# RMSNorm over 16,384 rows of 640 on one core: other tile sizes and row layout, scaling in place, a different share of squares, halved last stores

## The chip, the cores and the metric

One core of a Trainium2 chip runs the whole kernel. The metric is device time in microseconds of one execution, given as the median of several runs. The kernel before: 115.51 us, the median of 4 runs (115.45 to 115.58).

## What is computed

Every row of `x` (512 x 32 rows of 640 bf16 numbers) is divided by its root mean square and multiplied by a vector `g` of 640.

```python
B, S, D = 512, 32, 640
def reference(x, g):
    rms = jnp.sqrt((x * x).mean(axis=-1, keepdims=True) + 1e-6)
    return x / rms * g
```

`x` is 20.97 MB and the output as much; `g` is small.

## The kernel before

The 16,384 rows are cut into 16 tiles of 1,024 rows: 128 partitions with R = 8 rows each. A tile is one contiguous block of memory, 1.31 MB, of which a partition holds 10,240 contiguous bytes (lines 34 to 40). One Python loop over the tiles (line 62) is unrolled; a scheduler orders each engine's instructions at build time, mostly by program order, and puts in the semaphore waits. Each engine then works through its own list in that order. The work of one tile:

- SP issues the load of the tile into `x_sb` (line 66); the pool has 5 buffers, so the load of tile t+5 waits until tile t has been read for the last time.
- ACT (ScalarE) squares `kt` of the 8 rows, one instruction a row, which also sums the row into a column of `ms_a` in PSUM (line 73), and takes the root of these sums (line 80). `kt` follows the pattern 7, 7, 6, 7, 7, 7, 6, 7, which makes 108 rows of 128 per partition.
- DVE (VectorE) does the remaining `8 - kt` rows with a custom multiply-and-sum into `ms_d` (line 91), 20 in all; ACT takes their root as well (line 101).
- DVE takes the reciprocal of the 8 roots (line 108), multiplies the tile by `g` in two instructions of 4 rows into `xg` (line 113), and scales each row by its own reciprocal into `o_sb`, 8 instructions (line 122). `xg` has 2 buffers, `o_sb` has 3.
- POOL (GpSimd) issues the store of the tile, one DMA of 1.31 MB (line 130).

Before the loop ACT issues the load of `g`, broadcast to all partitions (line 52), and DVE writes the constant `eps_sb` (line 55).

All 16 DMA engines serve both the load queue of SP and the store queue of POOL.

Of the kernel before, what the change touches and what calls it, by code (L numbers as in the profile page):

```python
# [2 lines left out]

# [4 lines left out]


@with_exitstack  # L10
def kernel(
    ctx: ExitStack,
    tc: tile.TileContext,
    x: bass.AP,
    g: bass.AP,
    out: bass.AP,
):
    nc = tc.nc
    P = nc.NUM_PARTITIONS
    fp32 = mybir.dt.float32  # L20
    bf16 = mybir.dt.bfloat16
    Square = mybir.ActivationFunctionType.Square
    Sqrt = mybir.ActivationFunctionType.Sqrt
    mult = mybir.AluOpType.mult
    add = mybir.AluOpType.add

    xf = x.flatten_outer_dims()
    of = out.flatten_outer_dims()
    N, D = xf.shape
    assert N % P == 0  # L30
    rows_per_part = N // P
    eps = 1e-6

    R = 8
    while rows_per_part % R != 0:
        R -= 1
    T = rows_per_part // R

    xv = xf.rearrange("(t p r) d -> t p r d", p=P, r=R)
    ov = of.rearrange("(t p r) d -> t p r d", p=P, r=R)  # L40

    consts = ctx.enter_context(tc.tile_pool(name="consts", bufs=1))
    xpool = ctx.enter_context(tc.tile_pool(name="xpool", bufs=5))
    xgpool = ctx.enter_context(tc.tile_pool(name="xgpool", bufs=2))
    opool = ctx.enter_context(tc.tile_pool(name="opool", bufs=3))
    junkp = ctx.enter_context(tc.tile_pool(name="junk", bufs=2))
    psum_j = ctx.enter_context(tc.tile_pool(name="psum_j", bufs=2, space=bass.MemoryType.PSUM))
    psum_s = ctx.enter_context(tc.tile_pool(name="psum_s", bufs=2, space=bass.MemoryType.PSUM))
    statp = ctx.enter_context(tc.tile_pool(name="stats", bufs=3))

    g_sb = consts.tile([P, D], g.dtype, name="g_sb")
    nc.scalar.dma_start(out=g_sb[:], in_=g.partition_broadcast(P))

    eps_sb = consts.tile([P, 1], fp32, name="eps_sb")
    nc.vector.memset(eps_sb[:], eps)  # L55

    inv_sqrt_d = 1.0 / math.sqrt(D)
    inv_d = 1.0 / D

    kt_pattern = [7, 7, 6, 7, 7, 7, 6, 7]  # L60

    for t in range(T):
        kt = min(R, kt_pattern[t % len(kt_pattern)])
        nd = R - kt
        x_sb = xpool.tile([P, R, D], bf16, name="x_sb")
        nc.sync.dma_start(out=x_sb[:], in_=xv[t])

        rstd = statp.tile([P, R], fp32, name="rstd")
        if kt > 0:
            ms_a = psum_s.tile([P, R], fp32, name="ms_a")  # L70
            for r in range(kt):
                pj = psum_j.tile([P, D], fp32, name="pj")
                nc.scalar.activation(  # L73
                    out=pj[:],
                    in_=x_sb[:, r, :],
                    func=Square,
                    scale=inv_sqrt_d,
                    accum_out=ms_a[:, r : r + 1],
                )
            nc.scalar.activation(  # L80
                out=rstd[:, :kt],
                in_=ms_a[:, :kt],
                func=Sqrt,
                bias=eps_sb[:],
                scale=1.0,
            )
        if nd > 0:
            ms_d = statp.tile([P, R], fp32, name="ms_d")
            for r in range(kt, R):
                junk = junkp.tile([P, D], bf16, name="junk_dve")  # L90
                nc.vector.tensor_tensor_reduce(  # L91
                    out=junk[:],
                    in0=x_sb[:, r, :],
                    in1=x_sb[:, r, :],
                    scale=inv_d,
                    scalar=0.0,
                    op0=mult,
                    op1=add,
                    accum_out=ms_d[:, r : r + 1],
                )  # L100
            nc.scalar.activation(  # L101
                out=rstd[:, kt:R],
                in_=ms_d[:, kt:R],
                func=Sqrt,
                bias=eps_sb[:],
                scale=1.0,
            )
        nc.vector.reciprocal(out=rstd[:], in_=rstd[:])  # L108

        xg = xgpool.tile([P, R, D], bf16, name="xg")  # L110
        H = R // 2
        for h in range(2):
            nc.vector.tensor_tensor(  # L113
                out=xg[:, h * H : (h + 1) * H, :],
                in0=x_sb[:, h * H : (h + 1) * H, :],
                in1=g_sb[:, None, :].to_broadcast([P, H, D]),
                op=mult,
            )

        o_sb = opool.tile([P, R, D], bf16, name="o_sb")  # L120
        for r in range(R):
            nc.vector.tensor_scalar(  # L122
                out=o_sb[:, r, :],
                in0=xg[:, r, :],
                scalar1=rstd[:, r : r + 1],
                scalar2=None,
                op0=mult,
            )

        nc.gpsimd.dma_start(out=ov[t], in_=o_sb[:])  # L130


# [1 line left out]
_INS = ['x', 'g']  # L134
_OUTS = [((512, 32, 640), 'bfloat16')]


# [23 lines left out]
```

## Time and profile before

| | |
|---|---|
| median of 4 runs | 115.51 us (115.45 to 115.58) |
| the profiled execution's own time | 115.45 us |
| its span, first to last instruction | 113.7 us |
| DVE busy | 99.1 us, 217 instructions |
| ACT busy | 88.2 us, 250 instructions |
| POOL busy | 8.8 us, 20 instructions |
| moved by DMA | 42.14 MB |

All rows of the profile are from one execution, and their times count from the first instruction; 1.75 us of the execution's own time lie outside that span. A row of a timeline begins with its start and its duration in us, then engine, line, operation, output and input with their shapes, and a count where rows of one kind were merged; in brackets stands the idle time of the engine before it and what ended that. A row of a group has, behind the bar, the busy time in us and the mean duration of one in ns. A row of the waits says which engine waited for what: total us, times, and the longest where it is given. In the rows of 40 slices each digit is the busy share of one slice in tenths. PSUM and SBUF are the two on-chip memories; an engine name with a q behind it is that engine's queue.

### The profile page before, as it was taken

What the parts mean: (1) busy time and instruction counts of PE and PEld (TensorE: products, weight loads), DVE (VectorE), ACT (ScalarE), POOL (GpSimd) and SP (SyncE); (2) the same over time, 40 slices, a digit from 0 to 9 for tenths busy, and PEclk for the clock granted to TensorE, in tenths of its full rate; (3) what the DMA queues carried; (4) which work ended last, traced back from release to release, by engine and by line L of the source; (5) the groups of instructions that cost most, each with busy time, mean ns of one, the idle gap of its engine ahead of it and who ended that gap; (6) DMA issues with size and microseconds to landing.
All of it is one profiled execution on the core that took longest, in us unless ns stands there. A gap on an engine that the chain in (4) does not pass through costs nothing.

```text
span 113.7 us, 584 instructions
## 1 busy us (share of the span) xinstructions
DVE 99.1 (87%) x217; ACT 88.2 (78%) x250; POOL 8.8 (8%) x20
## 2 busy tenths in 40 slices
DVE  0019999999999999999999999999999999999700
ACT  4019999999999998989899999998989898710000
POOL 0000001101010101011010100101010101010100
DMA  4899999999999999999999999999999973809182
GB/s 66 313 352 440 414 443 422 436 422 428 404 418 435 425 436 422 432 429 418 436 425 436 429 429 429 424 429 407 425 425 436 414 335 126 346 0 404 58 346 115
DMA packets 4756, 42.14 MB, mean 371 GB/s; under 512 B 528, under 2 KB 656, under 8 KB 656
## 3 DMA queue, kind: packets, MB, share of 16 engines
q1 hardware_dynamic: 2304, 20.97, 44.8%
q0 software_dynamic: 2304, 20.97, 43.9%
q10 hardware_dynamic: 144, 0.16, 0.6%
q14 instruction: 4, 0.03, 0.1%
HBM read 21.14 MB, written 20.97 MB: 370 GB/s over the span
## 4 chain that ended last, share of the span: by engine, by line
issue 45%; DVE 26%; ACT 12%; DMA 6%; POOL 4%; POOLq 1%
DVE o_sb L122 13%; DVE xg L113 11%; ACT pj L73 10%; DMA x_sb<-in_x_dram 6%; POOL out_dram L130 4%; DVE junk_dve L91 2%; ACT L101 1%; DVE rstd L108 1%; POOLq L156 0%; ACT rstd L101 0%; ACT rstd L80 0%; DVE ms_d L91 0%; POOLq L130 0%
## 5 line engine op out<-in xcount | busy, mean ns | idle before, releaser
L73 ACT ACTIVATE pj<-x_sb 128x640 f32<-128x640 bf16 x108 | 76.1, 707 | 7.5 <-DMA x_sb<-in_x_dram 5.5
L113 DVE TENSOR_TENSOR xg<-x_sb,g_sb 128x2560 bf16<-128x2560 bf16 x32 | 46.7, 1472 | 0.0
L122 DVE TENSOR_SCALAR o_sb<-xg,rstd 128x640 bf16<-128x640 bf16 x128 | 39.3, 382 | 0.0
L91 DVE CUSTOM_DVE_ANT_0 junk_dve<-x_sb 128x640 bf16<-128x640 bf16 x20 | 16.1, 809 | 7.1 <-DMA x_sb<-in_x_dram 7.1
L130 POOL DMA_DIRECT2D out_dram<-o_sb x16 | 8.6, 540 | 98.9 <-DVE o_sb L122 98.9
L73 ACT ACTIVATION_READ_ACCUMULATOR pj<-x_sb 128x1 f32 x108 | 14.4, 133 | 0.0
L101 ACT ACTIVATE rstd<-ms_d,eps_sb 128x1 f32<-128x1 f32 (+1 forms) x16 | 4.8, 300 | 5.3 <-DVE ms_d L91 5.3
L80 ACT ACTIVATE rstd<-ms_a,eps_sb 128x7 f32<-128x7 f32 (+1 forms) x16 | 4.3, 267 | 0.0
L108 DVE RECIPROCAL rstd<-rstd 128x8 f32<-128x8 f32 x16 | 3.2, 198 | 0.2 <-ACT rstd L80 0.2
L73 ACT ACT_TABLE_LOAD x1 | 1.3, 1283 | 1.2 <-PEq L145 1.2
L91 DVE DVE_READ_ACCUMULATOR2_ANT ms_d<- 128x1 f32 x20 | 1.7, 84 | 0.0
L101 ACT ACT_TABLE_LOAD x1 | 1.3, 1283 | 0.0
L55 DVE MEMSET eps_sb<- 128x1 f32 x1 | 0.1, 59 | 0.8 <-PEq L145 0.8
L145 POOL MEMSET const-float32-0.0<- 128x1 f32 x1 | 0.1, 98 | 0.2 <-issue 0.2
L145 POOL MEMSET const-bfloat16-1.0<- 128x1 bf16 x1 | 0.1, 101 | 0.0
L145 POOL MEMSET const-float32-1.0<- 128x1 f32 x1 | 0.1, 98 | 0.0
L145 POOL MEMSET const-uint8-127<- 128x1 uint8 x1 | 0.1, 98 | 0.0
## 6 DMA issues: line engine op xcount, KB each, us to landing
x_sb<-in_x_dram SPq DMA_DIRECT2D x16, 1280.0 KB, 10.6
out_dram<-o_sb POOLq DMA_DIRECT2D x16, 1280.0 KB, 11.4
g_sb<-in_g_dram ACTq DMA_DIRECT2D x1, 160.0 KB, 7.4
```

What stands on the lines that cost most here:

```text
L55: nc.vector.memset(eps_sb[:], eps)
L73: nc.scalar.activation(out=pj[:], in_=x_sb[:, r, :], func=Square, scale=inv_sqrt_d, accum_out=ms_a[:, r : r + 1],)
L80: nc.scalar.activation(out=rstd[:, :kt], in_=ms_a[:, :kt], func=Sqrt, bias=eps_sb[:], scale=1.0,)
L91: nc.vector.tensor_tensor_reduce(out=junk[:], in0=x_sb[:, r, :], in1=x_sb[:, r, :], scale=inv_d, scalar=0.0, op0=mult, op1=add, accum_out= ...
L101: nc.scalar.activation(out=rstd[:, kt:R], in_=ms_d[:, kt:R], func=Sqrt, bias=eps_sb[:], scale=1.0,)
L108: nc.vector.reciprocal(out=rstd[:], in_=rstd[:])
L113: nc.vector.tensor_tensor(out=xg[:, h * H : (h + 1) * H, :], in0=x_sb[:, h * H : (h + 1) * H, :], in1=g_sb[:, None, :].to_broadcast([P, H, ...
L122: nc.vector.tensor_scalar(out=o_sb[:, r, :], in0=xg[:, r, :], scalar1=rstd[:, r : r + 1], scalar2=None, op0=mult,)
L130: nc.gpsimd.dma_start(out=ov[t], in_=o_sb[:])
L145: nc = _bacc.Bacc("TRN2", target_bir_lowering=False, num_devices=1)
```

## The change

- The rows are laid out otherwise: each partition now holds 128 consecutive rows of `x`, and a tile is a stretch of these. So a tile in memory is 128 pieces of 10,240 bytes, 163,840 bytes apart, for loads and stores alike.
- There are 17 tiles: 4 rows, 15 times 8, and 4 rows per partition.
- The pool of `x_sb` has 8 buffers instead of 5, that of `o_sb` 6 instead of 3; `xg` goes.
- A root of a single column is taken on ACT ahead of the loop.
- The rows that ACT squares follow a running share of 112/128, rounded: 4, then 6 and 8 in turn, and 4 for the last tile. Tiles in which ACT has all rows have no second root.
- The multiplication by `g` is one instruction per tile, into `o_sb`; the scaling reads and writes `o_sb` in place.
- The stores of the last three tiles are two DMAs each, of half the rows.

```diff
-    R = 8
-    while rows_per_part % R != 0:
-        R -= 1
-    T = rows_per_part // R
-
-    xv = xf.rearrange("(t p r) d -> t p r d", p=P, r=R)
-    ov = of.rearrange("(t p r) d -> t p r d", p=P, r=R)
+    xv = xf.rearrange("(p r) d -> p r d", p=P)
+    ov = of.rearrange("(p r) d -> p r d", p=P)
...
+        sizes = [4] + [8] * 15 + [4]
...
-    xpool = ctx.enter_context(tc.tile_pool(name="xpool", bufs=5))
-    xgpool = ctx.enter_context(tc.tile_pool(name="xgpool", bufs=2))
-    opool = ctx.enter_context(tc.tile_pool(name="opool", bufs=3))
+    xpool = ctx.enter_context(tc.tile_pool(name="xpool", bufs=8))
+    opool = ctx.enter_context(tc.tile_pool(name="opool", bufs=6))
...
+    warm = consts.tile([P, 1], fp32, name="warm")
+    nc.scalar.activation(out=warm[:], in_=eps_sb[:], func=Sqrt)
...
-    kt_pattern = [7, 7, 6, 7, 7, 7, 6, 7]
+    act_frac = 112.0 / 128.0
+    kt_list = []
+    acc = 0.0
+    done = 0
+    for s in sizes:
+        acc += s * act_frac
+        kt = int(round(acc)) - done
+        kt = max(0, min(s, kt))
+        kt_list.append(kt)
+        done += kt
...
-        x_sb = xpool.tile([P, R, D], bf16, name="x_sb")
-        nc.sync.dma_start(out=x_sb[:], in_=xv[t])
+        x_sb = xpool.tile([P, RMAX, D], bf16, name="x_sb")
...
+            nc.sync.dma_start(out=x_sb[:, :Rt, :], in_=xv[:, r0 : r0 + Rt, :])
...
-        xg = xgpool.tile([P, R, D], bf16, name="xg")
-        H = R // 2
-        for h in range(2):
+        o_sb = opool.tile([P, RMAX, D], bf16, name="o_sb")
+        CH = 8
+        for c0 in range(0, Rt, CH):
+            c1 = min(Rt, c0 + CH)
             nc.vector.tensor_tensor(
-                out=xg[:, h * H : (h + 1) * H, :],
-                in0=x_sb[:, h * H : (h + 1) * H, :],
-                in1=g_sb[:, None, :].to_broadcast([P, H, D]),
+                out=o_sb[:, c0:c1, :],
+                in0=x_sb[:, c0:c1, :],
+                in1=g_sb[:, None, :].to_broadcast([P, c1 - c0, D]),
                 op=mult,
             )
 
-        o_sb = opool.tile([P, R, D], bf16, name="o_sb")
-        for r in range(R):
+        for r in range(Rt):
             nc.vector.tensor_scalar(
                 out=o_sb[:, r, :],
-                in0=xg[:, r, :],
+                in0=o_sb[:, r, :],
                 scalar1=rstd[:, r : r + 1],
...
-        nc.gpsimd.dma_start(out=ov[t], in_=o_sb[:])
+        if t >= T - 3:
+            step = max(1, Rt // 2)
+            for c0 in range(0, Rt, step):
+                c1 = min(Rt, c0 + step)
+                nc.gpsimd.dma_start(out=ov[:, r0 + c0 : r0 + c1, :], in_=o_sb[:, c0:c1, :])
+        else:
+            nc.gpsimd.dma_start(out=ov[:, r0 : r0 + Rt, :], in_=o_sb[:, :Rt, :])
```

More of the change, by code (lines that the diff above doesn't have):

```diff
@@ L30 @@
     assert N % P == 0
-    rows_per_part = N // P
+    RP = N // P
     eps = 1e-6
-    R = 8
-    while rows_per_part % R != 0:
-        R -= 1
-    T = rows_per_part // R
-    xv = xf.rearrange("(t p r) d -> t p r d", p=P, r=R)
-    ov = of.rearrange("(t p r) d -> t p r d", p=P, r=R)
+    xv = xf.rearrange("(p r) d -> p r d", p=P)
+    ov = of.rearrange("(p r) d -> p r d", p=P)
+    RMAX = 8
+    if RP == 128:
+        head = [4]
+        tail = [8, 4]
+        rem = RP - sum(head) - sum(tail)
+        mid = []
+        while rem >= RMAX:
+            mid.append(RMAX)
+            rem -= RMAX
+        while rem > 0:
+            s = min(8, rem)
+            mid.append(s)
+            rem -= s
+        sizes = [4] + [8] * 15 + [4]
+    else:
+        sizes = []
+        rem = RP
+        while rem > 0:
+            s = min(8, rem)
+            sizes.append(s)
+            rem -= s
+    assert sum(sizes) == RP, sizes
+    T = len(sizes)
+    offsets = [sum(sizes[:i]) for i in range(T)]
     consts = ctx.enter_context(tc.tile_pool(name="consts", bufs=1))
-    xpool = ctx.enter_context(tc.tile_pool(name="xpool", bufs=5))
-    xgpool = ctx.enter_context(tc.tile_pool(name="xgpool", bufs=2))
-    opool = ctx.enter_context(tc.tile_pool(name="opool", bufs=3))
+    xpool = ctx.enter_context(tc.tile_pool(name="xpool", bufs=8))
+    opool = ctx.enter_context(tc.tile_pool(name="opool", bufs=6))
     junkp = ctx.enter_context(tc.tile_pool(name="junk", bufs=2))
@@ L87 @@
         if nd > 0:
-            ms_d = statp.tile([P, R], fp32, name="ms_d")
-            for r in range(kt, R):
+            ms_d = statp.tile([P, RMAX], fp32, name="ms_d")
+            for r in range(kt, Rt):
                 junk = junkp.tile([P, D], bf16, name="junk_dve")
@@ L101 @@
             nc.scalar.activation(
-                out=rstd[:, kt:R],
-                in_=ms_d[:, kt:R],
+                out=rstd[:, kt:Rt],
+                in_=ms_d[:, kt:Rt],
                 func=Sqrt,
@@ L107 @@
             )
-        nc.vector.reciprocal(out=rstd[:], in_=rstd[:])
-        xg = xgpool.tile([P, R, D], bf16, name="xg")
-        H = R // 2
-        for h in range(2):
+        nc.vector.reciprocal(out=rstd[:, :Rt], in_=rstd[:, :Rt])
+        o_sb = opool.tile([P, RMAX, D], bf16, name="o_sb")
+        CH = 8
+        for c0 in range(0, Rt, CH):
+            c1 = min(Rt, c0 + CH)
             nc.vector.tensor_tensor(
-                out=xg[:, h * H : (h + 1) * H, :],
-                in0=x_sb[:, h * H : (h + 1) * H, :],
-                in1=g_sb[:, None, :].to_broadcast([P, H, D]),
+                out=o_sb[:, c0:c1, :],
+                in0=x_sb[:, c0:c1, :],
+                in1=g_sb[:, None, :].to_broadcast([P, c1 - c0, D]),
                 op=mult,
             )
-        o_sb = opool.tile([P, R, D], bf16, name="o_sb")
-        for r in range(R):
+        for r in range(Rt):
             nc.vector.tensor_scalar(
                 out=o_sb[:, r, :],
-                in0=xg[:, r, :],
+                in0=o_sb[:, r, :],
                 scalar1=rstd[:, r : r + 1],
@@ L128 @@
             )
-        nc.gpsimd.dma_start(out=ov[t], in_=o_sb[:])
+        if t >= T - 3:
+            step = max(1, Rt // 2)
+            for c0 in range(0, Rt, step):
+                c1 = min(Rt, c0 + step)
+                nc.gpsimd.dma_start(out=ov[:, r0 + c0 : r0 + c1, :], in_=o_sb[:, c0:c1, :])
+        else:
+            nc.gpsimd.dma_start(out=ov[:, r0 : r0 + Rt, :], in_=o_sb[:, :Rt, :])
 _INS = ['x', 'g']
```

14 lines of the change are left out of this document (10 added, 4 removed).

## The prediction

> **What bounds the kernel now.** I read the page first: the engine totals, and the span in 40 slices.
>
> ```profile
> span 113.7 us, 584 instructions
> DVE 99.1 (87%) x217; ACT 88.2 (78%) x250; POOL 8.8 (8%) x20
> ...
> DVE  0019999999999999999999999999999999999700
> ACT  4019999999999998989899999998989898710000
> ...
> DMA  4899999999999999999999999999999973809182
> ...
> DMA packets 4756, 42.14 MB, mean 371 GB/s; under 512 B 528, under 2 KB 656, under 8 KB 656
> ```
>
> Two rows are full at once. DVE is at 9 from slice 3 to slice 36; DMA is at 9 from slice 2 to slice 31 and then falls apart into bursts, while DVE is still full. So the two must be told apart, by who waits:
>
> ```profile
> DVE junk_dve L91 <- DMA x_sb<-in_x_dram: 7.1, 1, 7.1
> ...
> ACT rstd L101 <- DVE ms_d L91: 5.3, 8, 3.1
> ...
> DVE rstd L108 <- ACT rstd L80: 0.2, 1, 0.2
> ```
>
> DVE waited for the first load (7.1 us) and 0.2 us once for ACT, and never again for a load. The DMA queues, though full, are always ahead. How far is in the next two rows (the last load's issue, its time to landing) and the first DVE read of that tile:
>
> ```profile
> 74.22 0.33 SPq L66 DMA_DIRECT2D x_sb<-in_x_dram  x1
> ```
> ```profile
> x_sb<-in_x_dram SPq DMA_DIRECT2D x1, 1280.0 KB, 12.2
> ```
> ```profile
> 101.13 0.82 DVE L91 CUSTOM_DVE_ANT_0 junk_dve<-x_sb 128x640 bf16<-128x640 bf16 x1
> ```
>
> The last tile landed at 74.22+12.2 = 86.4, and DVE touched it at 101.1. DVE is the bound. By how little the DMA engines are not, the windows say (columns: length, busy time of DVE, ACT and POOL with counts, clock, DMA share, GB/s):
>
> ```profile
> 0.00:5.00 5.00, 0.06 (x1) 1.28 (x1) 0.20 (x4) 1.00 0.66 185
> ...
> 0.00:8.00 8.00, 0.06 (x2) 1.29 (x2) 0.20 (x4) 1.00 0.75 233
> 8.00:19.50 11.50, 11.49 (x22) 11.22 (x29) 0.00 (x0) 1.00 1.01 429
> 19.50:89.00 69.50, 69.31 (x155) 66.35 (x194) 6.72 (x13) 1.00 1.01 426
> 89.00:113.70 24.70, 18.20 (x41) 9.38 (x27) 1.92 (x4) 1.00 0.56 232
> ```
>
> With loads alone (8 to 19.5) and with loads and stores mixed (19.5 to 89) the engines move the same 426 to 429 GB/s at a share of 1.01: that is their ceiling. By 8.0 us 233 x 8 = 1.86 MB have moved; the other 40.28 MB at 426 take 94.5 us, so the bytes alone can't be done before 102.5.
>
> The last rows that carry the sum are one whole tile on DVE and the end of the kernel:
>
> ```profile
> 52.50 2.89 DVE L113 TENSOR_TENSOR xg<-x_sb,g_sb 128x2560 bf16<-128x2560 bf16 x2
> 55.31 0.20 DVE L108 RECIPROCAL rstd<-rstd 128x8 f32<-128x8 f32 x1
> 55.42 0.78 DVE L91 CUSTOM_DVE_ANT_0 junk_dve<-x_sb 128x640 bf16<-128x640 bf16 x1
> ...
> 56.12 2.46 DVE L122 TENSOR_SCALAR o_sb<-xg,rstd 128x640 bf16<-128x640 bf16 x8
> 58.49 2.89 DVE L113 TENSOR_TENSOR xg<-x_sb,g_sb 128x2560 bf16<-128x2560 bf16 x2
> ```
> ```profile
> 104.75 2.46 DVE L122 TENSOR_SCALAR o_sb<-xg,rstd 128x640 bf16<-128x640 bf16 x8
> 107.50 0.53 POOL L130 DMA_DIRECT2D out_dram<-o_sb  x1 [5.46 <-DVE o_sb L122]
> ```
> ```profile
> 108.25:108.50 0.25, 0.00 (x0) 0.00 (x0) 0.00 (x0) 1.00 0.00 0
> 108.50:108.75 0.25, 0.00 (x0) 0.00 (x0) 0.00 (x0) 1.00 1.57 655
> ...
> 111.25:111.50 0.25, 0.00 (x0) 0.00 (x0) 0.00 (x0) 1.00 1.54 655
> 111.50:111.75 0.25, 0.00 (x0) 0.00 (x0) 0.00 (x0) 1.00 0.02 0
> ```
>
> Instructions overlap, so a cost is the distance from start to start: two multiplications by g 2.81 us, a reciprocal 0.11, a square on DVE 0.70, eight scalings 2.37. Sixteen tiles and 20 squares give 16 x 5.29 + 14.0 = 98.6, against the 99.2 us from 8.00 to the end of DVE (104.75+2.46 = 107.2). From there it is 6.5 us to the end: 0.3 to POOL's issue at 107.5, 1.0 to the first byte at 108.5, 3.0 for the 1.31 MB, 2.2 from the last byte to 113.7. The execution's own time is 115.45, so 1.75 us lie outside the span; the median of the runs (115.51) is 0.06 above it.
>
> **The change, part by part.**
>
> *Fewer squares on DVE.* The new rule gives the tiles 4, 6, 8, 6, 8 ... 6, 4 rows for ACT: 112 instead of 108, so DVE has 16 instead of 20. Less: 4 x 0.70 = 2.8 us. Whether ACT can pay for it:
>
> ```profile
> 21.24 0.27 ACT L80 ACTIVATE rstd<-ms_a,eps_sb 128x7 f32<-128x7 f32 x1
> 26.04 0.27 ACT L80 ACTIVATE rstd<-ms_a,eps_sb 128x6 f32<-128x6 f32 x1
> 31.64 0.27 ACT L80 ACTIVATE rstd<-ms_a,eps_sb 128x7 f32<-128x7 f32 x1
> ```
>
> A tile of 6 takes 4.80 us on ACT and one of 7 takes 5.60: 0.80 a square, roots hidden in it. 112 squares are 89.6 us. From a start at about 6 (below) ACT is done near 97 with the waits for tiles 0 and 1; DVE needs the last roots near 102. ACT keeps some 5 us of slack, and that cover is what makes the four squares free.
>
> *One multiplication per tile instead of two, into o_sb.* It saves one instruction's fixed part, 15 times. The trace has no row at 5,120 elements; the distance of 1.40 us holds at least its elements, and records overlap their neighbours by 1.49-1.40, so I bound the saving at 0 to 0.09 us and take 0.05: 0.75 us. The tile xg goes; DVE never waited for one, so nothing comes of that.
>
> *Scaling in place.* The same 128 instructions. Nearest row:
>
> ```profile
> L122 DVE TENSOR_SCALAR o_sb<-xg,rstd 128x640 bf16<-128x640 bf16 x128 | 39.3, 382 | 0.0
> ```
>
> A record lasts 382 ns, the distance is 2.37/8 = 296. If in-place writing forbade that overlap, it would cost 128 x 0.086 = 11.0 us; below zero there is no reason, since the same bytes are read and written. I take 0, since neighbouring instructions still touch different rows, as before; both ends are kept.
>
> *Seventeen tiles instead of sixteen:* one reciprocal more, 0.11. DVE's work is thus 99.2 - 2.8 - 0.75 + 0.1 = 95.8 us.
>
> *A first tile of 4 rows, and a root ahead of all.*
>
> ```profile
> x_sb<-in_x_dram SPq DMA_DIRECT2D x1, 1280.0 KB, 7.2
> ...
> g_sb<-in_g_dram ACTq DMA_DIRECT2D x1, 160.0 KB, 7.4
> ```
> ```profile
> 8.78 1.28 ACT L101 ACT_TABLE_LOAD   x1
> ```
>
> Tile 0 and g, both issued at 0.74, land at 7.9 and 8.1. Half a tile and g are 0.82 MB; 185 x 5 = 0.93 MB had moved by 5.0, so the half tile's bytes are in at 4.9 and it lands about 1 us later, near 5.9. ACT then has its 4 squares at 9.1, and the root's result at 9.4; the table load of 1.28, which DVE's own work covered before, would lie on this path, and the early root moves it into ACT's wait. DVE meanwhile can only multiply tile 0 (1.4 us), then waits for that root or for tile 1 (2.13 MB, near 9.6). If g lands with the half tile, DVE has done 1.4 us by 9.4; if g still lands at 8.1, DVE starts at 8.1 and waits for nothing. Either way it stands as if it had started at 8.0 to 8.1: the smaller first tile feeds ACT and the stores early, and gains DVE nothing. DVE ends at 8.1 + 95.8 = 103.9. For a wait at tile 2, whose 8 squares end on ACT at about 21.0 while DVE is through with its other work at 20.3, and others like it, I add 0.3: 104.2.
>
> *More buffers (8 and 6).* DVE had no wait for a buffer: 0. Stores start near 11 instead of 19.5 and take their share from the loads for 8 us longer, so the last loads land at about 92 instead of 86.4; DVE wants that tile after 101, ACT from 94. Cover enough, if the rate holds.
>
> *The stores of the last three tiles in halves.* The last one is 2 rows, 0.33 MB, 0.75 us instead of 3.0. Its first half is issued 0.6 us earlier and its 0.75 us of bytes overlap the second's first byte by 0.15. The tail is 6.5 - 2.25 + 0.15 = 4.4 us. Six POOL issues of 0.53 stand in place of three; the one ahead of the last is over when DVE ends. The Trainium skill, "SBUF — State Buffer", section "SBUF: two separate sides", says that a DMA issued from GpSimd can't write its descriptors while DVE runs an instruction in a two-port mode; no store of the trace was issued beside a scaling, so no run shows it yet. By it the first half's issue would end with the scalings, and the last would follow 0.5 us later than I have it.
>
> *Rows laid out as 128 consecutive ones per partition.* A load read one block of 1.31 MB; now it reads 128 pieces of 10 KB (5 KB for half tiles), 160 KB apart, and the stores write so. The trace has no such access. The bound above is the present 426 GB/s (the ceiling holds for reads alone and for the mix, so memory is not what sets it). Below, I can only bound it by the slowest stretch with queued loads, 185 GB/s over the first 5 us, which is start-up and far away; I take 426. The page "DMA: Bandwidth & Descriptors" of the Trainium skill, "Latency and other measured facts", speaks against this edit: a row pitch of a large power of two slowed copies, 207 GB/s at 512 KiB against 214 in full. By its 3% as an estimate the rate would be 412 GB/s, and the bytes would be done at 105.8, still just inside the sum below.
>
> *Sum.* DVE ends at 104.2, the tail is 4.4, the span 108.6; with 1.75 outside, **110.3 us**. Last bytes at 106.4, when at 426 GB/s all could be done at 102.5: the margin of the DMA engines is 4 us.
>
> **The rivals.**
>
> *DMA takes over, mildly.* The margin goes when 40.28 MB take longer than 106.4 - 8 = 98.4 us, below 409 GB/s (-4%). At 395 it is 8 + 102 + 2.2 + 1.75 = 114.0. For it: the share is 1.01 already, and DVE will ask for 16 rows each way (5.24 MB) in 95.8/8 = 12.0 us, 437 GB/s. Against: the loads' 12 us lead absorbs that. Chance 0.13.
>
> *Slower: the pitch costs over 9%.* The bytes then end after 111.5 (40.28 MB in 103.5 us: below 389 GB/s), and all that DVE gains is lost. At 370 it is 8 + 108.9 + 2.2 + 1.75 = 120.8. Against: each piece is still 10 KB long, and reading alone and mixing now reach the same ceiling. The Trainium skill's rule above grows with the pitch and gives 3% at three times this one. Chance 0.11. The in-place cost of 11 us (110.3 + 11 = 121.3) is the other way to end there: 0.02.
>
> *ACT and DVE wait for each other.* ACT's roots of the 8 tiles with two DVE squares stand in its queue ahead of the next tile's squares; DVE may get to those squares late. Now 8 such waits cost 5.3 us, 3.1 of it harmless at the end. If each of 8 cost 1.2 us, the 5 us of slack are gone and 4 to 5 come on top: about 114.5. Chance 0.10, of it 0.02 slower, 0.01 no change.
>
> *The tail does not shrink,* if halves wait for each other: 110.3 + 2.2 = 112.5. Chance 0.03.
>
> **How the numbers follow.** The forecast has 0.61. A measurement of this kernel can tell about 0.2% (0.23 us). Faster: 0.61 + 0.12 + 0.07 + 0.03 = 0.83; same 0.01 + 0.01 = 0.02 (the first from the mild rival); slower 0.11 + 0.02 + 0.02 = 0.15. The forecast's own range is 109.2 (0.09 saved on each multiplication, no waits, halves not in each other's way) to 111.5 (the multiplication saves nothing, the last issue comes one POOL issue of 0.53 later). Upward the range goes to 115.0, which leaves out 0.16; downward to 108.5.
>
> **What would show it.** Right: DVE busy near 96 us, ending at about 104 with under 3 us idle after its first instruction; 16 squares at L91's successor; scaling still 296 ns apart; first x landing near 6; DMA at 420 GB/s or more to about 90; 4.4 us after the last scaling. Wrong: a wait of DVE for a load late in the kernel, or GB/s below 409 while the share is 1 (pitch); scaling 382 ns apart (in place); ACT idle on DVE's squares by over 8 us.

## The result and the profile after

The changed kernel takes 112.17 us (median of 8 runs, 112.12 to 112.24; a ninth execution on record took 112.42) against 115.52 us (median of 13): a ratio of 0.971, 95% interval 0.970 to 0.972. It is 3.35 us faster; 5.2 had been forecast. The time lies above the forecast's own range (109.2 to 111.5) and inside the wider one, which goes to 115.0. The profiled execution has a span of 110.5 us.

From the page of the kernel after, the span, the totals and the same three rows of slices (DVE, ACT, DMA):

```profile
span 110.5 us, 563 instructions
...
DVE 95.3 (86%) x195; ACT 89.2 (81%) x251; POOL 12.0 (11%) x24
...
DVE  0053999999999999999999999999999999999600
ACT  5059999999998999799989999799999997990000
...
DMA  3999999999999999999999999999999993992692
```

DVE has 3.8 us less work, where 3.4 were forecast (95.8 us predicted, 95.3 measured). The DMA row still falls apart into bursts at its end. The groups show the parts of DVE's work:

```profile
L152 DVE TENSOR_TENSOR o_sb<-x_sb,g_sb 128x5120 bf16<-128x5120 bf16 (+1 forms) x17 | 44.7, 2632 | 6.0 <-DMA g_sb<-in_g_dram 6.0
L160 DVE TENSOR_SCALAR o_sb<-o_sb,rstd 128x640 bf16<-128x640 bf16 x128 | 39.3, 376 | 0.1
...
L129 DVE CUSTOM_DVE_ANT_0 junk_dve<-x_sb 128x640 bf16<-128x640 bf16 x16 | 12.6, 801 | 0.0
```

Sixteen squares for 20; the scalings cost the same 39.3 us in place. In the middle nothing has changed for the DMA engines, from the windows:

```profile
0.00:8.00 8.00, 1.18 (x2) 2.77 (x5) 0.20 (x4) 1.00 0.76 223
8.00:19.50 11.50, 9.64 (x16) 11.15 (x32) 0.67 (x1) 1.00 1.01 427
19.50:89.00 69.50, 69.50 (x142) 65.50 (x187) 6.38 (x12) 1.00 1.01 428
```

They move 427 and 428 GB/s, with pieces 160 KB apart. The difference to the forecast lies in the end. DVE's last rows in the timeline:

```profile
98.66 0.19 DVE L146 RECIPROCAL rstd<-rstd 128x8 f32<-128x8 f32 x1
98.78 1.43 DVE L152 TENSOR_TENSOR o_sb<-x_sb,g_sb 128x2560 bf16<-128x2560 bf16 x1
100.13 2.44 DVE L160 TENSOR_SCALAR o_sb<-o_sb,rstd 128x640 bf16<-128x640 bf16 x8
102.50 0.16 DVE L146 RECIPROCAL rstd<-rstd 128x4 f32<-128x4 f32 x1
102.70 1.27 DVE L160 TENSOR_SCALAR o_sb<-o_sb,rstd 128x640 bf16<-128x640 bf16 x4
```

DVE ends at 102.70 + 1.27 = 103.97; 104.2 was forecast. But the order is not the one I had assumed: the last tile's multiplication (98.78) stands ahead of the scalings of the tile before it (100.13), which therefore end at 102.6 instead of about 101.2. POOL's last issues, and what the DMA engines did then:

```profile
101.69 1.01 POOL L172 DMA_DIRECT2D out_dram<-o_sb  x1 [4.86 <-DVE o_sb L160]
102.87 0.63 POOL L172 DMA_DIRECT2D out_dram<-o_sb  x1 [0.17 <-DVE rstd L146]
103.67 1.14 POOL L172 DMA_DIRECT2D out_dram<-o_sb  x2 [0.18 <-issue]
```
```profile
100.00:103.25 3.25, 3.21 (x12) 0.00 (x0) 1.39 (x2) 1.00 0.03 11
103.25:108.25 5.00, 0.72 (x3) 0.00 (x0) 1.33 (x3) 1.00 1.01 392
108.50:110.50 2.00, 0.00 (x0) 0.00 (x0) 0.00 (x0) 1.00 0.00 0
```

For 3.25 us the engines are all but idle, then they are full for 5.0 us at 392 GB/s: 1.97 MB, which is the last full tile and the last tile together, 12 rows per partition. After the last byte 2.2 us pass to the end of the span. So the time now is: the first byte of the last full tile's store (103.25), plus 5.0, plus 2.2. DVE's last instruction isn't in this sum.

### The profile page after: what moved, and what is told of

Same layout as the page of the kernel before. It is cut to its first block, busy times and chain, and to the rows that moved or that the text cites. A ratio compares the mean times of both kernels' runs of the same rounds, so it can differ in the third digit from the quotient of the medians.

```text
span 110.5 us, 563 instructions
## 1 busy us (share of the span) xinstructions
DVE 95.3 (86%) x195; ACT 89.2 (81%) x251; POOL 12.0 (11%) x24
## 4 chain that ended last, share of the span: by engine, by line
issue 41%; DVE 37%; POOL 7%; DMA 5%; ACT 3%; POOLq 1%
DVE o_sb L152 17%; DVE o_sb L160 14%; DMA x_sb<-in_x_dram 5%; DVE junk_dve L129 5%; POOL out_dram L174 4%; POOL out_dram L172 3%; ACT pj L111 3%; DVE rstd L146 1%; POOLq L200 1%; ACT rstd L118 0%; POOLq L172 0%; POOLq L174 0%; DVE ms_d L129 0%
## 5 line engine op out<-in xcount | busy, mean ns | idle before, releaser
L111 ACT ACTIVATE pj<-x_sb 128x640 f32<-128x640 bf16 x112 | 78.9, 707 | 6.3 <-DMA x_sb<-in_x_dram 4.0
L152 DVE TENSOR_TENSOR o_sb<-x_sb,g_sb 128x5120 bf16<-128x5120 bf16 (+1 forms) x17 | 44.7, 2632 | 6.0 <-DMA g_sb<-in_g_dram 6.0
L160 DVE TENSOR_SCALAR o_sb<-o_sb,rstd 128x640 bf16<-128x640 bf16 x128 | 39.3, 376 | 0.1
L174 POOL DMA_DIRECT2D out_dram<-o_sb x14 | 7.6, 542 | 84.9 <-DVE o_sb L160 42.9
L129 DVE CUSTOM_DVE_ANT_0 junk_dve<-x_sb 128x640 bf16<-128x640 bf16 x16 | 12.6, 801 | 0.0
L172 POOL DMA_DIRECT2D out_dram<-o_sb x6 | 4.3, 710 | 7.6 <-DVE o_sb L160 7.1
L146 DVE RECIPROCAL rstd<-rstd 128x8 f32<-128x8 f32 (+1 forms) x17 | 3.2, 190 | 1.8 <-ACT rstd L118 1.8
L139 ACT ACTIVATE rstd<-ms_d,eps_sb 128x2 f32<-128x2 f32 x8 | 2.4, 296 | 2.9 <-DVE ms_d L129 2.9
L118 ACT ACTIVATE rstd<-ms_a,eps_sb 128x6 f32<-128x6 f32 (+2 forms) x17 | 4.5, 267 | 0.1
```

What stands on the lines that cost most here:

```text
L111: nc.scalar.activation(out=pj[:], in_=x_sb[:, r, :], func=Square, scale=inv_sqrt_d, accum_out=ms_a[:, r : r + 1],)
L118: nc.scalar.activation(out=rstd[:, :kt], in_=ms_a[:, :kt], func=Sqrt, bias=eps_sb[:], scale=1.0,)
L129: nc.vector.tensor_tensor_reduce(out=junk[:], in0=x_sb[:, r, :], in1=x_sb[:, r, :], scale=inv_d, scalar=0.0, op0=mult, op1=add, accum_out= ...
L139: nc.scalar.activation(out=rstd[:, kt:Rt], in_=ms_d[:, kt:Rt], func=Sqrt, bias=eps_sb[:], scale=1.0,)
L146: nc.vector.reciprocal(out=rstd[:, :Rt], in_=rstd[:, :Rt])
L152: nc.vector.tensor_tensor(out=o_sb[:, c0:c1, :], in0=x_sb[:, c0:c1, :], in1=g_sb[:, None, :].to_broadcast([P, c1 - c0, D]), op=mult,)
```

## The experiments

Each is the changed kernel with the edit shown. A theory of the tail (the stretch from DVE's last instruction to the end) stood behind the first four and the seventh: the bytes of the last 12 rows leave as one burst, and what sets the time is when the burst begins. The fifth and sixth were set up with the rival theory that DVE's work sets the end. The other rivals were the row pitch, the halves and the issues on POOL.

### Contiguous tiles again

```diff
+    def blk(f, r0, n):
+        return f[r0 * P : (r0 + n) * P, :].rearrange("(p r) d -> p r d", p=P)
-    ... in_=xv[:, r0 : r0 + Rt, :]
+    ... in_=blk(xf, r0, Rt)
```

> The changed kernel (112.17 us) with one edit: each tile is again one contiguous block of memory, for loads and stores; sizes, buffers, order and halved stores stay. Theory (the pitch costs nothing; the tail is long because the bytes of the last 12 rows queue up behind late stores): 112.0 to 112.4, 427 GB/s in the middle, the last bytes again near 108.3. Rival (pieces 160 KB apart slow the start and the end of the transfers): the first tile lands near 5.9 instead of 6.69, the last 1.97 MB move at 437 GB/s instead of 394, together 0.5 to 1.3 us less, 110.9 to 111.7.

Measured: 112.26 us (112.22 to 112.38), inside the theory's band, the order of every engine the same, 428 GB/s from 8 to 89 us, the first tile landing 6.1 us after its issue (5.9 with the pitch). The pitch costs nothing here, at either end. The page "DMA: Bandwidth & Descriptors" of the Trainium skill, "Latency and other measured facts", gives a loss for pitches of a power of two, from 512 KiB on. A pitch of 160 KB is smaller and no power of two, and this run shows no loss at it.

### Whole last stores

```diff
-        if t >= T - 3:
+        if False:
```

> The changed kernel with one edit: the stores of the last three tiles are whole again. Theory (the last 1.97 MB are one burst of DMA whatever their number): the store of the last full tile is issued after its last scaling, near 102.8, its first byte is near 103.8 instead of 103.25, so 0.3 to 0.6 us more: 112.5 to 112.8. Rival (the halves do what the prediction gave them, 2.1 us): 114.0 or more. Second rival (an issue beside the scalings is what holds the tail): equal or faster, up to 112.2.

Measured: 112.59 us (112.54 to 112.61). The issue of the last full tile starts at 102.81, the engines are full from 104.0 on:

```profile
104.00:108.75 4.75, 0.00 (x0) 0.00 (x0) 0.53 (x1) 1.00 1.01 414
```

These are the same 1.97 MB, in a burst that begins 0.75 us later and runs at 414 GB/s instead of 392. The theory's band holds: the halves gain 0.42 us here, not 2.1.

### The last multiplication behind the scalings

```diff
+        with tc.issue_after(last) if t == T - 1 else ExitStack():
             nc.vector.tensor_tensor(
                 out=o_sb[:, :Rt, :],
...
-            nc.vector.tensor_scalar(
+            last = nc.vector.tensor_scalar(
...
-            )
+            ).ins
```

> The changed kernel with one edit: the multiplication of the last tile is issued on DVE behind the scalings of the tile before it, not ahead of them. Theory (the order pushes the 1.31 MB of that tile 1.35 us back): its scalings end near 101.1 instead of 102.5, its bytes begin near 101.9 and are done near 105.0, DVE ends at 104.0 as before, the last bytes are near 106.5 to 107: 110.3 to 111.0. Rival (the issues on POOL set the tail): the last issue stays at 104.3, and the time at 111.8 or more.

Measured: 110.98 us (110.79 to 111.12), 1.2 less than the changed kernel and inside the theory's band. DVE's rows, POOL's issue of the last full tile's first half, and the DMA engines:

```profile
98.84 2.46 DVE L159 TENSOR_SCALAR o_sb<-o_sb,rstd 128x640 bf16<-128x640 bf16 x8
101.21 0.17 DVE L146 RECIPROCAL rstd<-rstd 128x4 f32<-128x4 f32 x1
101.30 1.46 DVE L151 TENSOR_TENSOR o_sb<-x_sb,g_sb 128x2560 bf16<-128x2560 bf16 x1
102.79 1.27 DVE L159 TENSOR_SCALAR o_sb<-o_sb,rstd 128x640 bf16<-128x640 bf16 x4
```
```profile
100.41 0.71 POOL L171 DMA_DIRECT2D out_dram<-o_sb  x1 [3.62 <-DVE o_sb L159]
```
```profile
101.50:107.00 5.50, 2.53 (x5) 0.00 (x0) 1.62 (x3) 1.00 0.91 358
```

DVE ends 0.1 us later than in the changed kernel (102.79 + 1.27 = 104.06), and the kernel is 1.2 us faster: DVE's end does not set the time, the start of the burst does. The last issue of POOL did stay near 104.3, as the rival said, but the time did not; that issue isn't the bound either. This is the order that the kernel before has and the prediction's sum assumes. With it the profiled execution has 109.1 - 104.06 = 5.0 us behind DVE's end, against 6.5 in the changed kernel and 4.4 in the forecast.

### Late stores on SP

```diff
-                nc.gpsimd.dma_start(out=ov[:, r0 + c0 : r0 + c1, :], ...
+                nc.sync.dma_start(out=ov[:, r0 + c0 : r0 + c1, :], ...
```

> The changed kernel with one edit: the halved stores of the last three tiles are issued by SP instead of POOL. Theory (most of the tail is the 1.97 MB from the first byte on; POOL's long issue beside the scalings delays that byte by some 0.5 us): 111.3 to 111.9, the first byte near 102.5 to 102.9. Rival (POOL's serial issues set the tail): 110.5 or less. Second rival (the issuing queue does not matter): 112.0 to 112.3.

Measured: 110.21 us (110.15 to 110.36), 2.0 less, better than my theory's band and inside the rival's. The trace shows that both had the sizes wrong:

```profile
101.32 0.33 SPq L172 DMA_DIRECT2D out_dram<-o_sb  x1
```
```profile
100.00:102.00 2.00, 2.00 (x8) 0.00 (x0) 0.00 (x0) 1.00 0.01 4
102.00:107.00 5.00, 1.84 (x7) 0.00 (x0) 0.00 (x0) 1.00 0.98 392
107.25:108.40 1.15, 0.00 (x0) 0.00 (x0) 0.00 (x0) 1.00 0.00 0
```

The burst is the same 5.0 us at 392 GB/s, so the issues on POOL do not set its length. It begins 1.2 us earlier: SP's issue starts at 101.32 and takes 0.33, POOL's started at 101.69 and took 1.01. (DVE itself is 0.1 us earlier in this run.) The rest, 0.8 us, is the time after the last byte: 1.4 instead of 2.2. I had expected neither that nor more than 0.5 of the first.

POOL's long issues stand beside the scalings. Two issues in a row in the kernel after, the first beside the scalings of 93.56 to 96.0, the second beside a multiplication:

```profile
95.12 1.01 POOL L172 DMA_DIRECT2D out_dram<-o_sb  x1 [2.21 <-DVE o_sb L160]
96.30 0.53 POOL L172 DMA_DIRECT2D out_dram<-o_sb  x1 [0.17 <-issue]
```

The Trainium skill, "SBUF — State Buffer", section "SBUF: two separate sides", states that a DMA of GpSimd cannot write its descriptors while DVE runs an instruction in a two-port mode. The trace fits that for the issues at 95.12 and 101.69, which end 0.1 us behind the scalings, and speaks against a full stop in other places. The issue at 102.87 took only 0.63 and ended inside the scalings. So did that of the third run at 100.41: it stands at the same place beside eight scalings (98.84 to 101.30), took 0.71 and ended 0.2 us ahead of their end. No run here separates the port from other reasons.

### The old share of squares

```diff
-    act_frac = 112.0 / 128.0
+    act_frac = 108.0 / 128.0
```

> The changed kernel (112.17 us) with one edit: the running share of ACT is 108/128 again, so DVE has 20 squares instead of 16 (one of them in the first tile). Theory (DVE's work sets the end): four squares of 0.70 to 0.75 us come back, of which the one in the first tile falls into DVE's wait of 1.8 us there: 2.1 to 3.0 us more, 114.3 to 115.2. Rival (the end is set by the transfers, DVE has room): 112.2 to 113.0.

Measured: 112.66 us (112.61 to 112.68), only 0.5 more, inside the rival's band. The theory as I had put it falls, though DVE has 3.0 us more work (98.3 against 95.3). The rival's reason, room on DVE, isn't shown by it either, since the order of the instructions has changed. The timeline:

```profile
100.33 2.46 DVE L160 TENSOR_SCALAR o_sb<-o_sb,rstd 128x640 bf16<-128x640 bf16 x8
102.70 0.17 DVE L146 RECIPROCAL rstd<-rstd 128x4 f32<-128x4 f32 x1
102.79 1.47 DVE L152 TENSOR_TENSOR o_sb<-x_sb,g_sb 128x2560 bf16<-128x2560 bf16 x1
104.29 1.27 DVE L160 TENSOR_SCALAR o_sb<-o_sb,rstd 128x640 bf16<-128x640 bf16 x4
```

DVE ends at 105.56, 1.6 later, but the scheduler here put the last multiplication behind the scalings. So the scalings of the last full tile begin at 100.33 instead of 100.13, and the burst 0.2 us later; the time is 0.5 longer. To see what the squares are worth, the order must be the same: against the third experiment, which has this order, it is 112.66 - 110.98 = 1.7 us (DVE's end: 105.56 - 104.06 = 1.5). That is four squares at 0.74, 3.0, less some 1.3 that fall into DVE's wait in the first tile (its wait for the first root is 0.5 us here instead of 1.8).

### Two multiplications per tile

```diff
-        CH = 8
+        CH = 4
```

> The changed kernel with one edit: the multiplication by g is two instructions of 4 rows again, still into o_sb. Theory (the starts of the changed kernel are 2.69 to 2.74 us apart where two halves took 2.81, and DVE sets the end): 15 x 0.07 to 0.12, 1.1 to 1.8 us more, 113.2 to 114.0. Rival (the prediction's own 0.05 each): 112.9. Second rival (nothing, the distance is the elements' alone): 112.1 to 112.4.

Measured: 111.96 us (111.94 to 112.24), no loss, and again none of the bands. Here too the scheduler put the last multiplication behind the scalings (99.90):

```profile
102.36 1.46 DVE L152 TENSOR_TENSOR o_sb<-x_sb,g_sb 128x2560 bf16<-128x2560 bf16 x1
```

So the edit's price is to be read against the third experiment: 111.96 - 110.98 = 1.0 us, or 0.065 for each of 15. DVE's busy time says the same: 96.3 us against 95.3.

### Sixteen even tiles

```diff
-        sizes = [4] + [8] * 15 + [4]
+        sizes = [8] * 16
```

> The changed kernel with one edit: 16 tiles of 8 rows, no tile of 4 at either end; ACT then has 7 of 8 rows in each tile. Theory (the small first tile gains DVE nothing, and the small last one only leaves bytes queued behind the tile before it): DVE ends near 104 again; the last 1.31 MB start near 104.4 and end near 107.6: 111.0 to 112.0. Rival (the small ends do gain, at the start 2 us or at the end 1 us): 113.0 to 115.0.

Measured: 112.09 us (112.03 to 112.16), just over the band of the theory. DVE's last instruction ends at 103.63, 0.3 us earlier than in the kernel after, so the small first tile gains DVE nothing, as forecast. The theory's account of the end did not hold: both last tiles, 2.62 MB, leave as one burst:

```profile
101.25:108.00 6.75, 2.38 (x8) 0.00 (x0) 1.90 (x3) 1.00 0.96 385
```

It ends 0.2 us ahead of that of the kernel after. In the order that the scheduler chose here, with the last multiplication ahead of both tiles' scalings, the two small tiles gain nothing; the other order was not run with even tiles.

### Product in a tile of its own

```diff
-                out=o_sb[:, c0:c1, :],
+                out=xg[:, c0:c1, :],
...
-                in0=o_sb[:, r, :],
+                in0=xg[:, r, :],
```

> The changed kernel with one edit: the product goes to a tile xg of its own (2 buffers) and the scaling reads that and writes o_sb, so nothing is done in place. Theory (in place costs nothing): scalings 296 ns apart in both, 111.9 to 112.5. Rival (in place costs overlap, or saves some): the distance of scalings differs and the time by over 1 us.

Measured: 112.55 us (112.53 to 112.64), 0.05 above the theory's band. The group of scalings:

```profile
L162 DVE TENSOR_SCALAR o_sb<-xg,rstd 128x640 bf16<-128x640 bf16 x128 | 39.3, 379 | 0.1
```

Eight of them take 2.37 us from start to start in both kernels: in place costs and saves nothing in the scalings. The 0.4 us more lie elsewhere: DVE's end comes 0.3 us later (104.26), its multiplications and reciprocals take 0.4 us more from start to start in all, and the scheduler has put them in another order. That the order alone is the cause was not tested.

### Without the early root

```diff
-    warm = consts.tile([P, 1], fp32, name="warm")
-    nc.scalar.activation(out=warm[:], in_=eps_sb[:], func=Sqrt)
```

> The changed kernel (112.17 us) without the root ahead of the loop. Theory (the table load of 1.28 us then stands between ACT's squares and the first root, on the path on which DVE waits 1.8 us): DVE's wait there grows to about 3.1 us, its whole row and the last store come 1.0 to 1.3 us later: 113.1 to 113.5. Rival (what DVE loses at the start it does not give to the end, since the transfers set it): 112.1 to 112.5.

Measured: 111.85 us (111.84 to 111.89), 0.3 less; neither had that. The table load does come late, but DVE does something else meanwhile:

```profile
9.96 0.82 DVE L127 CUSTOM_DVE_ANT_0 junk_dve<-x_sb 128x640 bf16<-128x640 bf16 x1 [1.60 <-DMA x_sb<-in_x_dram]
10.71 0.82 DVE L127 CUSTOM_DVE_ANT_0 junk_dve<-x_sb 128x640 bf16<-128x640 bf16 x1
10.74 1.28 ACT L116 ACT_TABLE_LOAD   x1
...
11.45 2.82 DVE L150 TENSOR_TENSOR o_sb<-x_sb,g_sb 128x5120 bf16<-128x5120 bf16 x1
```

In this kernel the scheduler placed the squares and the product of the second tile ahead of the first reciprocal. DVE waits 1.6 us for tile 1, in place of 1.8 for the root. What the early root is worth in an unchanged order was not measured.

### Both edits of the tail, then finer tiles, then fewer squares on DVE

The tenth run has the order of the third and the SP stores of the fourth. The eleventh cuts the last 12 rows in three and halves only the last store; order and SP then reach over these tiles. The twelfth gives ACT more squares.

```diff
-        sizes = [4] + [8] * 15 + [4]
+        sizes = [4] + [8] * 14 + [4, 4, 4]
...
-            step = max(1, Rt // 2)
+            step = Rt // 2 if t == T - 1 else Rt
...
-    act_frac = 112.0 / 128.0
+    act_frac = 115.0 / 128.0
```

> The changed kernel with two edits: the last multiplication issued behind the scalings of the tile before it, and the halved stores of the last three tiles issued by SP. Theory (the time is the first byte of the last full tile's store, 1.97 MB at about 395 GB/s or the last rows' own issue, whichever is later, and 1.35 us after the last byte): first byte near 100.8, that tile done near 104.1, the last half issued at 104.3, first byte near 105.1, last byte near 106.0: span 107.4, time 108.9 to 109.5. Rival (the two edits remove the same wait): 110.0 to 110.4.

> As the one before (order held by hand, late stores on SP), and the last 12 rows cut as three tiles of 4 where there was one of 8 and one of 4; only the last store is halved. Theory (the last bytes then follow the last scaling instead of queueing): 108.6 to 109.3, about one reciprocal later on DVE (104.1). Rival (the two edits had emptied the queue already): no less than 109.2.

> As the one before, with a running share of 115/128 of the squares on ACT, 3 fewer on DVE. Theory (with the queue empty at the end DVE's work sets the time, and ACT has about 4 us of slack): 3 x 0.72 = 2.2 us less, 106.5 to 107.3. Rival (ACT becomes the bound, or the DMA engines: 42.14 MB at 427 GB/s end no earlier than 102.5): 107.5 to 109.

Measured: 109.18 us (109.09 to 109.22), 109.37 (109.33 to 109.57) and 108.45 (108.35 to 108.52). The first is inside the theory's band; the two edits nearly add up, 3.0 us for the pair against 1.2 and 2.0. Its windows:

```profile
100.75:104.25 3.50, 3.21 (x8) 0.00 (x0) 0.00 (x0) 1.00 0.93 375
104.25:106.00 1.75, 0.00 (x0) 0.00 (x0) 0.00 (x0) 1.00 0.98 375
106.00:107.30 1.30, 0.00 (x0) 0.00 (x0) 0.00 (x0) 1.00 0.00 0
```

The burst begins at 100.8; the last bytes now do follow DVE's end, which is at 103.99, by 2.0 us. The finer tiles gain nothing on that (the rival): DVE ends at 104.41 there, not at 104.1, and the last byte again comes 2.0 us behind it. With three squares fewer on DVE, 0.9 us came, not 2.2. DVE's last row and the windows:

```profile
101.19 1.27 DVE L159 TENSOR_SCALAR o_sb<-o_sb,rstd 128x640 bf16<-128x640 bf16 x4
```
```profile
8.00:89.00 81.00, 79.11 (x155) 78.98 (x229) 6.51 (x12) 1.00 1.00 425
98.00:104.75 6.75, 4.40 (x12) 1.00 (x3) 0.00 (x0) 1.00 1.00 404
```

Now the DMA engines are full from 98 us to the last byte, at 404 GB/s, while DVE's last scaling ends at 102.5. The transfers bound the end, as the rival had it, but not from the start on: from 88.5 to 90.25 the engines moved only 35 GB/s, and the next store was issued only at 89.16; that gap and the lower rate behind it put the last bytes near 105 instead of 102.5. This is the fastest version run: a ratio of 0.939 to the kernel before, interval 0.938 to 0.940.

## Why the prediction was right, and what failed

The direction was right, and DVE's end (104.2 forecast, 103.97 measured). The time came 1.9 us above the forecast, because the tail did not shrink. Part by part:

- *DVE is the bound before, with no wait for a load.* Held: with less work DVE ends 107.2 - 104.0 = 3.2 us earlier, and in the same order of the tail work put back on DVE costs time (1.7 and 1.0 us by the fifth and sixth runs against the third). That its last instruction alone sets the end was too simple. That 3.2 us is close to the whole gain of 3.35 is chance: the tail is 6.5 us in both kernels, but made up differently. Before it was 0.3 + 1.0 + 3.0 + 2.2; after, a burst that starts 0.7 us ahead of DVE's end and lasts 5.0, and then 2.2.
- *DVE's work, 95.8 us.* It was 95.3. The squares saved 3.0 us where 2.8 were forecast (16.1 to 12.6 us of busy time is 3.5, part of it overlap); the multiplications saved 1.0 by the sixth against the third run, where 0.75 were forecast.
- *Start as if at 8.0 to 8.1.* Missed by 0.6 us. The first tile landed near 6.7 instead of 5.9, when 141 and not 185 GB/s had come in the first 5 us (124 in the first run, so this isn't the pitch). DVE's wait for the root was of the forecast kind:

```profile
6.88 1.49 DVE L152 TENSOR_TENSOR o_sb<-x_sb,g_sb 128x2560 bf16<-128x2560 bf16 x1 [6.00 <-DMA g_sb<-in_g_dram]
10.20 0.18 DVE L146 RECIPROCAL rstd<-rstd 128x4 f32<-128x4 f32 x1 [1.83 <-ACT rstd L118]
```

A start at 6.88 and a wait of 1.83 stand for a start at 8.7. DVE's end came out within 0.2 us because this 0.6 was made up by 0.5 us less work and by the 0.3 for other waits, of which none came. So far the number was luck.

- *The early root keeps 1.28 us off the path.* Not borne out: without it the kernel is 0.3 us faster, in another order of DVE's instructions.
- *In place, pitch, buffers: nothing.* Held, by the eighth run for the scalings and by the first for the pitch. The number of buffers was not varied.
- *The tail, 6.5 - 2.25 + 0.15 = 4.4 us.* This is the step that failed: 110.5 - 103.97 = 6.5, not a tenth gained. I had let the last full tile's bytes be gone when the last tile's came. In the run its first half left at 103.25, because the last multiplication came ahead of its scalings (1.2 us by the third run) and because POOL's issue, beside them, let the first byte go later than SP's does (1.2 us by the fourth). So 1.97 MB stood in line where I had counted the last 0.33. With the order that I had assumed, the third run has a tail of 5.0, so 1.2 (by the medians) to 1.5 of the missing 2.1 us hang on the order. The rule of the Trainium skill on GpSimd's descriptors, as weighed in the prediction ("SBUF — State Buffer", "SBUF: two separate sides"), put 0.5 us on the last issue; that issue started at 104.27, 0.3 us behind DVE's end, as without the rule.
- *A margin of 4 us for the DMA engines.* The rate bears it out (428 GB/s up to 89 us), but it is a margin of the whole run. At the end what counts is the bytes not yet released: the engines idled for 3.25 us and then were late.
- *The rival "the tail does not shrink" (112.5, chance 0.03).* Its time is the nearest to the measured one, but its reason did not come: the halves ran back to back with the engines full (share 1.01), and whole stores are 0.42 us slower (second run). The prediction weighed no other reason for it.
- *The rivals of the DMA rate, of the pitch, and of ACT and DVE waiting for each other.* None came: 428 GB/s up to 89 us at a pitch of 160 KB, above the 409 and 389 below which the first two begin, and ACT waited for DVE's squares 2.9 us in all.

What remains open: why the scheduler orders the last instructions differently when something far from them changes, what lengthens POOL's issue beside scalings in some places and not in others, and what makes the time after the last byte 0.8 us longer with POOL's stores than with SP's.

## What to carry to other kernels

A sum over an engine's work forecasts when that engine ends, not when the kernel does: for the end, write down when each of the last stores is released, and queue their bytes at the measured rate. Before reading the price of an edit, look whether the order of the last instructions is the same in both kernels; two of these edits hid a loss of 1.0 and 1.7 us behind a better order. Here the DMA engines idled for 3.25 us just before the last burst, and the two edits that let it begin earlier were worth 1.2 and 2.0 us.

## What was not expected of the hardware

- An issue on POOL beside DVE's scalings took 1.01 us instead of 0.53, twice, and 0.63 at another place of the same kernel; in the third run it took 0.71 where the kernel after has the second 1.01.
- The first byte came 0.8 us after the start of SP's issue and 1.6 us after POOL's at the same place. From the end of POOL's issue it was about 0.5 us each time: 108.03 to 108.5 in the kernel before, 101.12 to 101.65 in the third run, 102.70 to 103.25 in the kernel after. From the last byte to the end of the span it was 1.4 us with SP and 2.2 with POOL.
- Stores of 2 and 4 rows ran at 392 GB/s, whole ones of 8 and 4 rows at 414.
